# Early score maxima of a fused FNet and multi-query kernel: two key blocks folded into one pass for five query tiles

## Chip, core and metric

The kernel runs on one core of a Trainium2 chip. The metric is the device time of one execution in microseconds. Before the change the median of three runs is 3697.52 us (3696.55 to 3697.98).

## What is computed

Two identical layers, each an FNet mixing sublayer (A) and a multi-query attention sublayer (B), over 2048 rows of 512 numbers:

```python
x = x + A(layernorm(x))   # y = Re(DFT_seq(DFT_hidden(x))): a = x Wre', b = x Wim'; y = Cre a - Cim b
x = x + B(layernorm(x))   # 32 query heads of 16, one key head, one value head
# B: scores = q k' / 4; p = softmax(scores); o = p v; o wo
```

The softmax subtracts the row maximum, so for each of 32 heads and 2048 queries the maximum over 2048 keys is needed before the exponentials.

## The kernel before

**Phase A** of a layer forms the DFT over the sequence for four blocks of 512 output rows. A block is 32 steps: 16 sequence chunks for the real matrix and 16 for the imaginary one. In each step one chunk of the DFT matrix (`craw`, loaded by SP) is split into a high part `ch` (ScalarE, ACT, line 80) and a low part `cl` (GpSimd, POOL, line 81), and TensorE (PE) multiplies it into four PSUM accumulators `x`. From step 48 on (`ROWS`) these matmuls are written as halves of 64 rows (line 650), two of which run side by side; a step is four slots of three such pairs. After 32 steps comes the y stage (line 456 in the halved form), eight units long, with four slots each, and then the preparation of the finished block, spread over the next twelve steps (`prep_tasks`): layer norm, four transposes, keys and values (`do_kv`), and four query projections `q_mm` in the steps 7 to 10 of the next block. Each projection is split into two rows of SBUF, `row4` and `row5` for groups 0 and 2, `row6` and `row7` for 1 and 3, and `q_store` writes these to DRAM (`qd`) with six DMAs one step later (line 347).

**Early maxima.** Since the keys of a finished block are known while later blocks are still in phase A, a part of the row maxima is taken there. The unit of it is a tile of 128 queries and a block of 512 keys: 16 head pairs, for each pair two matmuls (line 361) into PSUM banks `y` and two `reduce_max` on VectorE (DVE, line 362). The table `EARLY` lists (query tile, key block, SBUF slot for the queries, step of their load, start, end). Start and end count 40 positions for a block: 32 steps and the eight y units. The 16 head pairs are placed evenly between them. The banks are `y` (three buffers), `z` (one buffer, also used by the transposes) and `x` (two pairs). Maxima go to `mxe`, for tile 0 straight to its `mxp`.

**Phase B** runs 16 query tiles of 32 steps. A step has four score matmuls (line 817), two exponentials of 1024 columns on ACT (line 820), eight value matmuls in two groups of four (line 831), and some of the maxima not yet taken: `owed(n)` paces them at three a step. They use lines 361 and 362 as well, and write `mxp`.

All engines execute their own instructions in the order of the program. A buffer that is allocated again waits, at its first writer, for every reader of its earlier use, a DMA too, even one that stands later in the program text.

## Time and profile before

| | |
|---|---|
| median of three runs | 3697.52 us |
| the profiled execution | 3699.45 us, span 3697.7 us, granted clock 0.996 |
| layer 1, phase A | about 0 to 700 us |
| layer 1, phase B | about 700 to 1850 us |
| layer 2, phase A | about 1850 to 2500 us |
| layer 2, phase B | about 2500 to 3697 us |
| busy, of the span | PE 98%, DVE 76%, ACT 64%, POOL 25% |

In the views that follow, a row of groups gives line, engine, operation, output and inputs, shapes and count, then busy time and mean nanoseconds of one, then the idle time of the engine just ahead and what ended it. PEld is the weight load of a matmul. A row of the timeline gives start, length, engine, line, operation, tiles and how many follow each other. Reported matmul lengths overlap, so PE's pace is read from starts.

### The profile page before, as it was taken

Reading aid. Unit: us, or ns where it says so; the run is one execution under the profiler, and the core shown is the slowest. Engines: PE = TensorE matmul, PEld = TensorE weight load, DVE = VectorE, ACT = ScalarE, POOL = GpSimd, SP = SyncE. Lnnn points to the kernel's source line nnn. Section 1 sums busy time; section 2 is a strip of 40 time slices with the busy share of each in tenths; the row PEclk is TensorE's granted clock in tenths of the full one; section 3 lists DMA queues with packets and bytes.
Section 4 is the critical chain, followed back from the end, with each engine's and each line's share of the span. In section 5 each row is a group of like instructions: output and inputs, shape, how many; then the busy total and the mean of one; then the engine's idle time right before and its main releaser. Section 6 shows DMA issues by size and latency. Waiting matters only on the chain.

```text
span 3697.7 us, 63649 instructions
## 1 busy us (share of the span) xinstructions
PE 3612.1 (98%) x24672; PEld 1822.8 (49%) x24672; DVE 2817.3 (76%) x4847; ACT 2363.3 (64%) x2974; POOL 915.5 (25%) x1288
## 2 busy tenths in 40 slices
PE   8999999999999999999999999998999999999999
PEld 6866567533333333333377666675333333333333
DVE  6176988688888888888411879886888888888882
ACT  3322221488888888888933231215888888888888
POOL 5534332212112212211254342322111011010101
PEclk9999999999999999999999999999999999999999
DMA  6534233311111100110144242423111111001101
GB/s 189 137 122 148 69 109 92 97 34 34 50 33 36 48 22 25 33 50 22 42 138 121 97 142 69 132 69 101 33 48 36 33 45 39 25 22 47 36 22 27
DMA packets 218047, 247.17 MB, mean 67 GB/s; under 512 B 51664, under 2 KB 173584, under 8 KB 210064
## 3 DMA queue, kind: packets, MB, share of 16 engines
q1 hardware_dynamic: 204048, 225.78, 20.5%
q0 software_dynamic: 13696, 17.33, 1.7%
q8 instruction: 194, 3.18, 0.4%
q14 instruction: 109, 0.89, 0.1%
HBM read 178.77 MB, written 63.17 MB: 65 GB/s over the span
## 4 chain that ended last, share of the span: by engine, by line
PE 90%; DVE 6%; ACT 2%; issue 1%; POOL 1%; DMA 0%; SPq 0%; ACTq 0%; DVEq 0%; POOLq 0%
PE z L831 27%; PE y L361 18%; PE x L817 18%; PE x L650 9%; PE x L456 3%; DVE mxe L362 3%; PE y L89 3%; PE y L91 2%; PE y L90 2%; PE x L91 2%; PE x L90 2%; PE x L89 2%; DVE mxp L362 1%; ACT slot L820 1%; DVE row L183 0%
## 5 line engine op out<-in xcount | busy, mean ns | idle before, releaser
L362 DVE TENSOR_REDUCE mxp<-y 128x1 f32<-128x512 f32 (+1 forms) x3168 | 1972.0, 679 | 229.1 <-PE y L361 208.0
L820 ACT ACTIVATE slot<-x 128x1024 f32<-128x1024 f32 x1990 | 1938.3, 1025 | 295.5 <-PE x L817 278.5
L831 PE MATMUL z<-slot,v 128*32 128x512 f32 x8192 | 1098.0, 606 | 1.5 <-DVE row L835 0.7
L361 PE MATMUL y<-kz,slot 64*128 64x512 f32 (+1 forms) x3360 | 1043.2, 407 | 36.5 <-DVE mxe L362 20.8
L817 PE MATMUL x<-slot,kz 64*128 64x512 f32 x2956 | 675.2, 451 | 9.7 <-DMA slot<-mt 5.8
L362 DVE TENSOR_REDUCE mxe<-y 128x1 f32<-128x512 f32 x960 | 584.3, 682 | 96.2 <-PE y L361 89.2
L817 PEld LDWEIGHTS x<-slot,kz 64*128 64x128 f32 x2956 | 278.5, 184 | 751.8 <-ACT slot L820 677.3
L361 PEld LDWEIGHTS y<-kz,slot 64*128 64x128 f32 x3360 | 484.5, 185 | 236.0 <-DVE mxe L362 166.3
L650 PE MATMUL x<-ch,xnh 64*128 64x512 f32 (+1 forms) x1536 | 411.6, 371 | 5.6 <-DVE row L438 4.2
L650 PE MATMUL x<-ch,xnl 64*128 64x512 f32 (+1 forms) x1536 | 411.3, 371 | 0.0
L650 PE MATMUL x<-cl,xnh 64*128 64x512 f32 (+1 forms) x1536 | 391.4, 354 | 0.0
L81 POOL TENSOR_TENSOR cl<-craw,ch 128x512 fp32r<-128x512 f32 x236 | 300.9, 1297 | 259.4 <-ACT ch L80 232.2
L831 PEld LDWEIGHTS z<-slot,v 128*32 128x32 f32 x8192 | 164.0, 108 | 359.3 <-issue 328.9
L443 ACT CAST xnl<-xnl 128x2 fp32r<-128x2 f32 x160 | 31.2, 195 | 473.6 <-PE x L650 276.4
L650 PEld LDWEIGHTS x<-cl,xnh 64*128 64x128 f32 x1536 | 248.8, 185 | 19.3
L410 POOL DMA_DIRECT2D slot<-mt x208 | 103.3, 504 | 612.8 <-PE y L361 518.8
L650 PEld LDWEIGHTS x<-ch,xnh 64*128 64x128 f32 x1536 | 233.9, 185 | 28.8 <-issue 6.6
L650 PEld LDWEIGHTS x<-ch,xnl 64*128 64x128 f32 x1536 | 234.3, 185 | 19.5 <-issue 4.5
L872 POOL TENSOR_TENSOR row<-row,row 128x256 f32<-128x256 f32 x63 | 46.6, 739 | 686.2 <-DMA row<-rd 661.9
L80 ACT CAST ch<-craw 128x512 fp32r<-128x512 f32 x256 | 147.8, 618 | 39.5 <-DMA craw<-ct_in 13.9
L89 PE MATMUL x<-ch,xnh 128*128 128x512 f32 x384 | 154.8, 403 | 12.2 <-ACT ch L80 9.0
L91 PE MATMUL x<-ch,xnl 128*128 128x512 f32 x384 | 153.5, 400 | 2.0 <-POOL xnl L518 1.8
(168 smaller groups left out, 3131.0 us busy)
## 6 DMA issues: line engine op xcount, KB each, us to landing
craw<-ct_in SPq DMA_DIRECT2D x112, 512.0 KB
slot<-qd SPq DMA_DIRECT2D x48, 1024.0 KB
qd<-row SPq DMA_DIRECT2D x144, 128.0 KB
od<-row SPq DMA_DIRECT2D x252, 64.0 KB
row<-x_in SPq DMA_DIRECT2D x32, 256.0 KB
mid<-row POOLq DMA_DIRECT2D x32, 256.0 KB, 2.3
craw<-ct_in SPq DMA_DIRECT2D x32, 256.0 KB
row<-mid SPq DMA_DIRECT2D x32, 256.0 KB
```

Source lines behind the costliest of these rows:

```text
L80: nc.scalar.copy(hi, raw)
L81: (eng or nc.vector).tensor_sub(lo, raw, f(hi))
L89: nc.tensor.matmul(ps_, ah, bh, start=start, stop=False)
L90: nc.tensor.matmul(ps_, ah, bl, start=False, stop=False)
L91: nc.tensor.matmul(ps_, al, bh, start=False, stop=stop)
L361: nc.tensor.matmul(pm, o.qT[i][gs, pr, :], kz[gs, c0:c0 + n], start=True, stop=True)
L362: nc.vector.reduce_max(to, pm, axis=AX.X)
L456: nc.tensor.matmul(y[:, g ^ h, :], a[cc][gs, k, tt * P:(tt + 1) * P], b[cc][gs, k, :], start=(h, cc, k, u) == (0, 0, 0, 0), stop=(h, cc, k ...
L650: nc.tensor.matmul(z[d], a[gs, s, d * P:(d + 1) * P], b[gs, :], start=first and q < 2 and e == 0, stop=last and q > 1 and e == len(order) - 1)
L817: nc.tensor.matmul(st["e"][:, g, :], kz[64 * g:64 * g + KR, c * P:(c + 1) * P], o.qT[i][64 * g:64 * g + KR, cp:cp + 4, :], start=True, sto ...
L820: nc.scalar.activation(ptiles[i, s_][:, 2 * w:2 * w + 2, :], st.pop("e"), AF.Exp, scale=DH ** -0.5)
L831: nc.tensor.matmul(a[32 * j:32 * j + 32, :], v1[:, c, :], pt[:, j, :], start=c == 0, stop=c == NT - 1)
```

## The change

1. Five query tiles (0, 4, 5, 6, 7) take key blocks 0 and 1 in one go, entries `"f"` of the table. With a difference of keys `kd` = keys of block 0 minus keys of block 1, max(a, b) = b + max(a - b, 0): PE forms a - b into two `y` banks and b into a `y` and the `z` bank, ACT rectifies a - b into `row4` and `row5`, and DVE adds b and takes the maximum in one pass (`tensor_tensor_reduce`). The number of matmuls is the same.
2. `k_diff` forms `kd` once per layer, behind the keys of block 1.
3. The table is rewritten: 12 entries instead of 18, with other starts, ends, slots and loads. Seven single tiles and five folded ones make 17 tiles of maxima in place of 18; (2, 2) goes to phase B. Tile (3, 1) now lies among the folded ones, from 87.25 to 109. Single maxima of odd head pairs use `z` for one of their two banks.
4. The split of the query weights moves from POOL to DVE, has buffers `wh` and `wl` of its own, and is issued behind the projection instead of ahead of it. `ch` and `cl` have four buffers instead of six.
5. Phase B starts with 8 maxima owed instead of 6 and adds one for every 32 steps. Slots for `zh` and `zl` are taken one step later in some places, and the row maxima of tile 14 are made in two halves.

```diff
@@ -33,12 +33,10 @@
 
 
 EARLY = [
-    (0, 0, 2, 44, 56, 61.5), (1, 0, 3, 44, 61.5, 66.5), (2, 0, 2, 54, 66.5, 70.9), (3, 0, 8, 50, 70.9, 87),
-    (0, 1, 0, 66, 87, 91), (1, 1, 1, 66, 91, 94.7), (3, 1, 8, None, 94.7, 98.7),
-    (4, 0, 2, 78, 98.7, 102.7), (4, 1, 2, None, 102.7, 106.7), (5, 0, 3, 78, 106.7, 110.7),
-    (6, 0, 8, 84, 110.7, 116), (6, 1, 8, None, 116, 122.5), (7, 0, 0, 97, 122.5, 126.5),
-    (7, 1, 0, None, 126.5, 130.5), (5, 1, 1, 97, 130.5, 134.6), (2, 1, 2, 108, 134.6, 138.6),
-    (2, 2, 2, None, 138.6, 142.6), (0, 2, 8, 101, 142.6, 148.5),
+    (1, 0, 2, 44, 56, 63.5), (2, 0, 3, 44, 63.5, 70.9), (3, 0, 8, 50, 70.9, 86.5),
+    (0, "f", 0, 66, 87, 95), (3, 1, 8, None, 87.25, 109), (4, "f", 2, 78, 95.5, 103), (5, "f", 3, 78, 103, 110.9),
+    (6, "f", 8, 95, 114, 122), (1, 1, 1, 97, 122.5, 128), (2, 1, 0, 97, 128, 133.9),
+    (7, "f", 2, 108, 134.5, 142.5), (0, 2, 8, 101, 142.5, 148.5),
 ]
 ROWS = 48
 KEPT = [e for e in EARLY if e[0]]
@@ -121,7 +119,7 @@
         return sb.tile([P, 2, 512], F32, name="craw", bufs=3)
 
     def hl_tiles():
-        return (sb.tile([P, 512], F32R, name="ch", bufs=6), sb.tile([P, 512], F32R, name="cl", bufs=6))
+        return (sb.tile([P, 512], F32R, name="ch", bufs=4), sb.tile([P, 512], F32R, name="cl", bufs=4))
 
     wkvh = sb.tile([P, NK, P], F32R, name="wkvh")
     wkvl = sb.tile([P, NK, P], F32R, name="wkvl")
@@ -236,8 +234,8 @@
             nc.sync.dma_start(st["wq", g], wq[:, g, :])
 
         def wq_split(g):
-            st["wqh", g] = hl_tiles()
-            split_sb(st["wq", g], *st["wqh", g], nc.gpsimd)
+            st["wqh", g] = sb.tile([P, 512], F32R, name="wh"), sb.tile([P, 512], F32R, name="wl")
+            split_sb(st["wq", g], *st["wqh", g])
 
         def wq_split_pool(g):
             hi, lo = st["wqh", g] = hl_tiles()
@@ -273,6 +271,19 @@
             for g in range(2):
                 gs = slice(64 * g + 32, 64 * g + 48)
                 nc.vector.tensor_sub(kz[gs, cs], st["pk"][gs], f(kz[gs, cs]))
+
+        def k_diff(tb):
+            if tb == 0:
+                st["kraw"] = sb.tile([P, 512], F32, name="kraw")
+                nc.scalar.copy(st["kraw"], st["pk"])
+                return
+            st["kd"] = kd = sb.tile([P, 512], F32R, name="kd")
+            t = st["kraw"]
+            nc.vector.tensor_sub(t, t, st["pk"])
+            nc.scalar.activation(kd, t, AF.Identity, scale=kmask)
+            for g in range(2):
+                gs = slice(64 * g + 32, 64 * g + 48)
+                nc.vector.tensor_sub(kd[gs], t[gs], f(kd[gs]))
 
         def v_tr(t0, n, vt):
             pv_ = bank("z")[:, :n * 32].rearrange("p (t d) -> p t d", t=n)
@@ -351,23 +362,42 @@
             if i not in o.mxp:
                 o.mxp[i] = sb.tile([P, NPAIR, 2, 4 if i else 5], F32, name=f"mxp{i % 4}")
                 for e, (i_, kb, *_) in enumerate(KEPT):
-                    if i == i_:
-                        nc.gpsimd.tensor_copy(o.mxp[i][:, :, :, kb], st["mxe"][:, e])
+                    for k in (0, 1) if kb == "f" else (kb,):
+                        if i == i_:
+                            nc.gpsimd.tensor_copy(o.mxp[i][:, :, :, k], st["mxe"][:, e])
             return o.mxp[i]
 
-        def max_of(i, pr, g, c0, n, to):
-            pm = bank("y")[:, :n]
+        def max_of(i, pr, g, c0, n, to, tag="y"):
+            pm = bank(tag)[:, :n]
             gs = slice(64 * g, 64 * g + KR)
             nc.tensor.matmul(pm, o.qT[i][gs, pr, :], kz[gs, c0:c0 + n], start=True, stop=True)
             nc.vector.reduce_max(to, pm, axis=AX.X)
+
+        def max_two(i, pr, to):
+            rows = [half(4 + g) for g in range(2)]
+            for k, c in ((st["kd"], 0), (kz, 512)):
+                pm = [bank("z" if c and g else "y") for g in range(2)]
+                for g in range(2):
+                    gs = slice(64 * g, 64 * g + KR)
+                    nc.tensor.matmul(pm[g], o.qT[i][gs, pr, :], k[gs, c:c + 512], start=True, stop=True)
+                for g in range(2):
+                    if c:
+                        nc.vector.tensor_tensor_reduce(rows[g], pm[g], rows[g], 1.0, -3.0e38, ALU.add, ALU.max, to[:, g:g + 1])
+                    else:
+                        nc.scalar.activation(rows[g], pm[g], AF.Relu)
 
         def max_early(e, pr):
             i, kb = EARLY[e][:2]
             if "mxe" not in st:
                 st["mxe"] = sb.tile([P, len(KEPT), NPAIR, 2], F32, name="mxe")
+            if kb == "f":
+                max_two(i, pr, st["mxe"][:, KEPT.index(EARLY[e]), pr] if i else partial(0)[:, pr, :, 0])
+                if i == 0 and pr == NPAIR - 1:
+                    nc.gpsimd.tensor_copy(partial(0)[:, :, :, 1], partial(0)[:, :, :, 0])
+                return
             for g in range(2):
                 to = st["mxe"][:, KEPT.index(EARLY[e]), pr, g:g + 1] if i else partial(0)[:, pr, g, kb:kb + 1]
-                max_of(i, pr, g, kb * 512, 512, to)
+                max_of(i, pr, g, kb * 512, 512, to, "z" if pr % 2 and g else "y")
 
         def max_half(i, pr, g, kb):
             max_of(i, pr, g, kb * 512, 512, partial(i)[:, pr, g, kb:kb + 1])
@@ -562,12 +592,12 @@
             ts[4, 1] = [lambda: tr(2)]
             ts[4] = [lambda: tr(3), lambda: [wq_load(g) for g in range(4)]]
             ts[6, 0] = [do_kv]
-            ts[6, 3] = [lambda: kv_lo(4 * tb, 4)]
+            ts[6, 3] = [lambda: (kv_lo(4 * tb, 4), k_diff(tb) if tb < 2 else None)]
             ts[6] = [lambda: wq_split(0), lambda: v_tr(4 * tb, 4, st["vt"])]
             for g in range(4):
                 ts[7 + g] = [lambda g=g: q_mm(tb, g, *st["xt"])]
                 if g < 3:
-                    ts[7 + g].insert(0, lambda g=g: wq_split(g + 1))
+                    ts[7 + g].append(lambda g=g: wq_split(g + 1))
                 if g:
                     ts[7 + g].append(lambda g=g: q_store(tb, g - 1))
             ts[11] = [lambda: q_store(tb, 3)]
@@ -713,7 +743,7 @@
                     for tt in range(4):
                         x1[tt] = half(tt)
                         nc.sync.dma_start(x1[tt], src[4 * tb + tt])
-                if n in (15, 31, 47, 62, 78, 94, 110, 118):
+                if n in (15, 31, 47, 63, 79, 95, 111, 119):
                     zh[c] = slot(2 * c, F32R).rearrange("p (k t) -> p k t", k=NK)
                     zl[c] = slot(2 * c + 1, F32R).rearrange("p (k t) -> p k t", k=NK)
                 if n < ROWS:
@@ -778,7 +808,7 @@
             for k in range(6):
                 more_max()
 
-        early = {e[:2] for e in EARLY}
+        early = {(e[0], kb) for e in EARLY for kb in ((0, 1) if e[1] == "f" else e[1:2])}
         units = [(0, pr, g, 3) for pr in range(HALF, NPAIR) for g in range(2)]
         units += [(i, pr, g, kb) for i in range(1, NT) for pr in range(NPAIR) for kb in range(4) for g in range(2)
                   if (i, kb) not in early]
@@ -790,7 +820,7 @@
                 o.done += 1
 
         def owed(n):
-            return min(3 * (n + 1) + 6, len(units)) - o.done
+            return min(3 * (n + 1) + 8 + max(n - 13, 0) // NSTEP, len(units)) - o.done
 
         def done_with(i, pr):
             return all(u[:2] > (i, pr) for u in units[o.done:])
@@ -1010,8 +1040,8 @@
                             o.loaded.add(j)
                 for fn in half_tasks(i).get(s_, ()):
                     fn()
-                for at, j, p0, np_ in ((NT - AHEAD, i, HALF, HALF), (NSTEP - AHEAD, i + 1, 0, HALF if i == NT - 2 else NPAIR)):
-                    if j in (0, NT - 1) or j == i + 1 < NT:
+                for at, j, p0, np_ in ((NT - AHEAD, i, HALF, HALF), (NSTEP - AHEAD, i + 1, 0, HALF if i >= NT - 3 else NPAIR)):
+                    if j in (0, NT - 2, NT - 1) or j == i + 1 < NT:
                         if s_ == at:
                             assert done_with(j, p0 + np_ - 1)
                             max_neg_a(j, p0, np_)
```

PE's order near the start of the second half of block 2's steps, before. `y` and `x` are PSUM, `slot2` holds queries of tile 4, `kz` the keys; each L650 row is one pair of halves:

```order
L361 MATMUL y_3832<-kz_70,slot2_3604 128x512
L361 MATMUL y_3835<-kz_70,slot2_3604 128x512
L650 MATMUL x_3678<-ch_3674,xnl_84 128x512 x2
L650 MATMUL x_3678<-cl_3675,xnh_83 128x512 x2
L650 MATMUL x_3678<-ch_3674,xnh_83 128x512 x2
L361 MATMUL y_3844<-kz_70,slot2_3604 128x512
L361 MATMUL y_3847<-kz_70,slot2_3604 128x512
```

Of the change, the same tile, with one head pair of the single tile (3, 1), whose queries are in `slot8`:

```order
L382 MATMUL y_3669<-kd_2937,slot2_3566 128x512
L382 MATMUL y_3670<-kd_2937,slot2_3566 128x512
L382 MATMUL y_3675<-kz_70,slot2_3566 128x512
L382 MATMUL z_3676<-kz_70,slot2_3566 128x512
L680 MATMUL x_3653<-ch_3497,xnh_83 128x512 x2
L680 MATMUL x_3653<-cl_3498,xnh_83 128x512 x2
L680 MATMUL x_3653<-ch_3497,xnl_84 128x512 x2
L680 MATMUL x_3653<-ch_3501,xnh_83 128x512 x2
L680 MATMUL x_3653<-cl_3502,xnh_83 128x512 x2
L680 MATMUL x_3653<-ch_3501,xnl_84 128x512 x2
L373 MATMUL y_3694<-kz_70,slot8_1766 128x512
L373 MATMUL z_3697<-kz_70,slot8_1766 128x512
```

Before, each slot ends with one head pair of one key block; now every second slot ends with one head pair of two key blocks, whose last matmul needs the only `z` bank.

ACT's order in the change at the first two query projections of block 1, with what each instruction waits for (`row4_2991` and `row5_2992` belong to a folded head pair, `row4_3024` is the high part of a projection, DMAHW are DMAs that must have landed):

```order
L387 ACTIVATE row4_2991<-y_2993 128x512 [waits PE_49]
L387 ACTIVATE row5_2992<-y_2994 128x512 [waits PE_49]
L82 ACTIVATE row0_3026<-y_3011 128x512 [waits PE_49,Activation_49]
L83 CAST row4_3024<-row0_3026 128x512 [waits DVE_49,Activation_49]
L78 CAST wh_3030<-row1_2847 128x512 [waits DMAHW0_49]
L78 CAST ch_3036<-craw_2785 128x512 [waits DMAHW6_49]
L78 CAST ch_3040<-craw_2785 128x512
L387 ACTIVATE row4_3050<-y_3052 128x512 [waits DMAHW2_49,DMAHW5_49,DMAHW1_49,DMAHW6_49,PE_49,Pool_49]
L387 ACTIVATE row5_3051<-y_3053 128x512 [waits DMAHW0_49,DMAHW7_49,DVE_49,PE_49]
```

Before, nothing but casts stood behind the projection's split; now the rectify that follows it writes `row4` again and waits for the six DMAs of `q_store`. The same holds two projections later.

On DVE one folded head pair is four instructions, two passes and behind each the read of its maximum:

```order
L385 ISA row4_2991,mxp0_2958<-y_2999,row4_2991 128x512
L385 ISA mxp0_2958 128x1
L385 ISA row5_2992,mxp0_2958<-z_3000,row5_2992 128x512
L385 ISA mxp0_2958 128x1
```

These take the place of four `reduce_max` of 128x512.

## Prediction

> **What bounds the kernel now.** First the page's busy line and its slices.

> ```profile
> PE 3612.1 (98%) x24672; PEld 1822.8 (49%) x24672; DVE 2817.3 (76%) x4847; ACT 2363.3 (64%) x2974; POOL 915.5 (25%) x1288
> ...
> PE   8999999999999999999999999998999999999999
> DVE  6176988688888888888411879886888888888882
> ```

> PE looks full everywhere, so the share says nothing about who sets the pace. The groups do: the weight loads of the maxima's matmuls wait for the reductions, most in phase A (`mxe`).

> ```profile
> L361 PEld LDWEIGHTS y<-kz,slot 64*128 64x128 f32 x3360 | 484.5, 185 | 236.0 <-DVE mxe L362 166.3 <-DVE mxp L362 42.9 <-DVE row L893 7.0
> ```

> Next the paces, from two timelines of phase A: PE where maxima are sparse (with the DVE row there), and DVE where they are dense.

> ```profile
> 262.40 0.40 PE L361 MATMUL y<-kz,slot 64*128 64x512 f32 x2
> 262.64 2.92 PE L456 MATMUL x<-slot,slot 64*128 64x512 f32 x24
> 265.39 0.40 PE L361 MATMUL y<-kz,slot 64*128 64x512 f32 x2
> ...
> 262.83 1.29 DVE L362 TENSOR_REDUCE mxe<-y 128x1 f32<-128x512 f32 x2 [2.36 <-PE y L361]
> ...
> 351.72 6.66 DVE L362 TENSOR_REDUCE mxe<-y 128x1 f32<-128x512 f32 x11
> ```

> Thirteen pairs of halves take 265.39 - 262.40 = 2.99 us, 0.23 a pair: a slot of three pairs is 0.69. A result reaches DVE 0.43 after its matmul's start. Reductions follow each other every (6.66 - 0.68) / 10 = 0.60. One head pair in every slot asks 1.20 of DVE and 0.92 of PE, so in dense stretches DVE sets the pace. The windows of line 362 (length, DVE busy, count; 32 a tile) show where:

> ```profile
> 195.40:256.30 60.90, 58.40 (x97) 1.00 0.37 131
> 256.30:316.40 60.10, 20.55 (x33) 0.97 0.30 106
> 316.40:368.80 52.40, 40.18 (x67) 1.00 0.52 141
> 368.80:446.40 77.60, 76.13 (x128) 1.00 0.24 82
> 446.40:496.70 50.30, 38.79 (x64) 0.97 0.21 74
> 496.70:574.50 77.80, 58.76 (x97) 1.00 0.47 129
> 574.50:614.40 39.90, 38.43 (x66) 1.00 0.25 81
> ```

> By their counts these stretches are the table's positions 56, 70.9, 87, 95, 110.7, 122.5, 134.6 and 142.6. I price layer 1 and double it.

> **The folded head pair.** No row shows the combined pass. The nearest are these:

> ```profile
> L438 DVE TENSOR_TENSOR row<-y,row 128x512 f32<-128x512 f32 x12 | 8.3, 692 | 87.9 <-PE y L91 87.9
> L81 DVE TENSOR_TENSOR slot<-row,slot 128x512 fp32r<-128x512 f32 x16 | 16.4, 1035 | 25.1 <-ACT slot L80 25.1
> L942 DVE TENSOR_SCALAR lnv<-mv 128x1 f32<-128x1 f32 x16 | 2.3, 145 | 0.0
> L84 ACT ACTIVATE row<-y 128x512 f32<-128x512 f32 x24 | 14.4, 599 | 109.6 <-issue 82.7 <-PE y L91 13.9 <-POOL cl L81 13.0
> ```

> The pass adds PSUM to SBUF as L438 does: 0.69, started 0.60 apart as reductions are. The read of its maximum I take as 0.10, between nothing and L942's 0.145. DVE needs 1.4 a head pair for two key blocks, where four reductions need 2.4. That gain is real, but the new work is a chain and `z` is one buffer. From the first matmul at 0: rectifies 0.43 to 1.03 and, 0.52 later (two casts of 0.62 in 1.14, below), to 1.55; first pass 1.06 to 1.75; second 1.76 to 2.45, its read to 2.55. Only then is `z` free, and PE, being in order, holds two slots (1.38) behind the next head pair's last matmul. A late bank also exposes a weight load, 0.19 by the group above and 0.05 of handover. With period p, that matmul starts at 2.55 - p + 0.24 and ends 0.23 later, and the next head pair follows 1.38 after that: p = 1.38 + 0.23 + 0.24 + 2.55 - p, **p = 2.2** against 1.84 (eight pairs) at PE's pace and 2.4 before. With the read free it is 2.15; without overlap of passes, and 0.15 for the read, 2.3.

> [...]

> A single head pair among folded ones (tile (3, 1)) puts two reductions, 1.20, between the passes and delays a bank by that plus 0.24: 1.44, where PE alone would need 0.23.

> **The waits for `q_store`.** The first folded tile lies on positions 87 to 95, where the four projections of block 1 are. Before, there:

> ```profile
> 320.27 0.47 PE L89 MATMUL y<-slot,ch 128*128 128x512 f32 x1 [0.20 <-DVE mxp L362]
> ...
> 323.18 0.50 PE L650 MATMUL x<-ch,xnh 64*128 64x512 f32 x2
> ...
> 323.33 0.60 ACT L84 ACTIVATE row<-y 128x512 f32<-128x512 f32 x1 [6.90 <-issue]
> 323.97 0.62 ACT L85 CAST row<-row 128x512 fp32r<-128x512 f32 x1
> 324.49 1.14 ACT L80 CAST ch<-craw 128x512 fp32r<-128x512 f32 x2
> ...
> 324.61 3.94 SPq L347 DMA_DIRECT2D qd<-row  x6
> ...
> mid<-row POOLq DMA_DIRECT2D x32, 256.0 KB, 2.3
> ...
> qd<-kz POOLq DMA_DIRECT2D x32, 128.0 KB, 3.8
> ```

> A projection takes 2.9 on PE. Its six DMAs are all issued 5.4 after its end (328.55 - 323.18), and land, by the two nearest rows, 2.3 to 3.8 later. The rectify behind it writes `row4` and waits for them: 7.7, then 0.60 and 0.24 until PE has a bank, 8.5 in all. On ACT every later cast and rectify stands behind it, on DVE the passes and reductions, and PE runs out of `y` banks after three slots and one head pair, some 2.5. So PE stands 6 us, twice (groups 0 and 2): 12, between 0 (if other waits cover it) and 15. SP runs ahead and is not held.

> **The sum for a layer.**
> - Positions 56 to 70.9: two single tiles in 59.6 slots, 41.1 + 32 x 0.23 = 48.5 at PE's pace, some 50 with uneven spacing, DVE 38: -11.
> - 87 to 95: 16 x 2.2 + four projections 11.6 + six singles 8.6 + 12 = 67.4 against 52.4: +15.
> - 95 to 110.9: 32 x 2.2 + 12 x 1.44 = 87.7 against 77.6: +10. Before, 3.9 tiles of one key block stood here; now it is 4.7.
> - 110.7 to 122.5: 14.4 slots 9.9 + 16 x 2.2 = 35.2, and 3 for the row sums of the y stage that enter DVE between the passes: 48 against 50.3: -2.
> - 122.5 to 134.6: two single tiles instead of three, with 285 halves 32.8, 60 full matmuls 13.8, transposes 2, maxima 7.4 on PE, and 8 kept for the preparation's waits: 64 against 77.8: -14.
> - 134.6 to 142.6: 16 x 2.2 + 1 = 36 against 39.9: -4.
> - `kd`: behind the keys of block 1 come a subtraction (0.69), a scaling and two small subtractions before the first folded matmul:

> ```profile
> L262 ACT ACTIVATE kz<-y,kone,kmask 128x512 fp32r<-128x512 f32 (+1 forms) x10 | 6.9, 694 | 38.0 <-PE y L91 38.0
> L275 DVE TENSOR_TENSOR kz<-y,kz 16x512 fp32r<-16x512 f32 (+1 forms) x20 | 11.7, 584 | 48.7 <-ACT row L265 48.4
> ```

>   0.69 + 0.69 + 2 x 0.58 = 2.6 later than the keys alone; about 2 of it is uncovered: +2.
> - Casts of `ch` (1.14 every two steps) stand ahead of rectifies; I take 0.05 a folded head pair: +4. The weight split behind the projection has one buffer, with a step (2.8) to cover some 2.9: +1. Four instead of six `ch` buffers still leave two steps for 1.2 of casts and 2.6 of POOL: 0. POOL's eight subtractions less, the later `zh` and the copies of `mxe` lie beside other work: 0.
> - Phase B gets tile (2, 2), 32 maxima more. Its step, before:

> ```profile
> 1299.99 0.40 PE L817 MATMUL x<-xnh,kz 64*128 64x512 f32 x2
> 1300.24 0.39 PE L361 MATMUL y<-kz,slot 64*128 64x512 f32 x1
> 1300.56 1.07 PE L831 MATMUL z<-slot,v 128*32 128x512 f32 x8
> ...
> 1301.56 0.50 PE L817 MATMUL x<-xnh,kz 64*128 64x512 f32 x2
> ```

>   The third maximum runs alone for 0.32, so a fourth beside it costs little; 16 pairs of 0.23 are 3.7: +4, from 0 to 32 x 0.60 = 19 if DVE set the pace there.

> Together -11 + 15 + 10 - 2 - 14 - 4 + 2 + 4 + 1 + 4 = **+5 a layer, +10 in all**. The profiled execution took 3699.45 us (span 3697.7), so it would be 3709; the median shown is 2 lower, so **3708 us**. The spread of single tiles wins, the folded tiles where a fifth one is squeezed in lose it again. The sum is even at p = 2.2 - 5/80 = 2.14, close by.

> **Rivals.**
> - *The chain is hidden* (other side: not slower). If `z` came free within 1.83 of the head pair's first matmul instead of 2.55 (2 x 1.84 - 1.38 - 0.23 - 0.24 = 1.83), PE would not stop and p would be 1.84; below 2.14 the change wins. For it speaks DVE's load, 1.4 in 1.84; against it the single `z` buffer and the order of PE. Then 87 to 95 takes 42.5 (-10), 95 to 110.9 61 (-16), 110.7 on 42 (-8), 134.6 on 29.5 (-10); with -11, -14, +2 and +4: -63 a layer, 3572; with the `q_store` waits kept -51, 3596. Chance 12%; in between, 3615 to 3680, 14%.
> - *The pass is dearer*: if it costs L81's 1.035 instead of 0.69, the chain is 0.69 longer, p 2.55, 80 head pairs a layer 28 more: 3763. 12%. For it: L81 adds two tensors and is that slow at times. Against: L438 reads PSUM, as the pass does, and is not. [...]
> - *More than one of these, or later landings of `q_store`*: above 3740, 7%.

> **How the numbers follow.** The forecast (3680 to 3740) has 55%, of it 5% below 3690, 15% up to 3705, 35% above. 0.2%, 7.4 us, is about what a measurement of this kernel tells from no change. Faster: 12 + 14 + 5 = 31%; the same 15%; slower 35 + 12 + 7 = 54%. The range leaves out the strongest gain and the worst sums: 3615 to 3775.

> **What would show it.** In the changed profile: combined passes of 0.69 and reads near 0.10; between folded head pairs starts 2.2 apart with weight loads of line 382 waiting for DVE; two idle stretches of some 6 us on ACT's line 387 that end with `qd` landing, around the projections; 56 to 70.9 in 50 us; phase B 4 us longer. Folded head pairs 1.84 apart, or no waits at `row4`, would make the forecast wrong.

## The result, and the profile after

The changed kernel takes 3729.51 us (median of 4 runs, 3726.0 to 3735.91) where the kernel before takes 3697.68 (3696.55 to 3697.98): ratio 1.0089, 95% interval 1.0071 to 1.0106. It is slower by 32 us; 3708 was forecast, with a range of 3615 to 3775.

The page of the changed kernel, its busy line and the granted clock in slices:

```profile
PE 3597.7 (96%) x24672; PEld 1864.2 (50%) x24672; DVE 2681.5 (72%) x4885; ACT 2544.0 (68%) x3288; POOL 899.2 (24%) x1280
...
PEclk9998999999999999999999989999999999999999
```

VectorE has less to do (72% for 76%), ScalarE more (68% for 64%), as the fold intends. TensorE is busy 14 us less in a span that is 32 longer. The mean granted clock of the profiled execution is 0.986 over a span of 3729.8 us; before it was 0.996 over 3697.7. Time at missing clock is (1 - 0.986) x 3729.8 = 52 us against 15. Not all of that costs time (PE waits in some of it anyway), but it is more than the whole loss, and no term of the prediction speaks of it. The four runs of the changed kernel rank by their clock: 3726.0 us at 0.989, 3727.42 at 0.988, 3731.59 at 0.986 and 3735.91 at 0.985.

Where the time went is read by cutting phase A at the same steps in both traces (a block is 32 steps and eight y units, so that step 71 is position 87, step 79 is 95, step 98 about 122.5, step 110 about 134):

| stretch | before, layers 1 and 2 | after, layers 1 and 2 | difference | forecast |
|---|---|---|---|---|
| steps 48 to 63 (two spread single tiles) | 62.2, 62.2 | 50.5, 50.5 | -11.7, -11.7 | -11 |
| 71 to 79 (first fold, four projections) | 52.8, 52.8 | 75.1, 75.2 | +22.3, +22.4 | +15 |
| 79 to 95 (folds with tile (3, 1)) | 77.8, 77.8 | 79.4, 79.4 | +1.6, +1.6 | +10 |
| 95 to 98 with the y stage | 47.2, 46.0 | 45.2, 46.6 | -2.0, +0.6 | -2 |
| 98 to 110 (single tiles, preparation) | 77.4, 77.3 | 74.4, 78.8 | -3.0, +1.5 | -14 |
| 110 to 120 | 61.3, 61.3 | 56.7, 58.7 | -4.6, -2.6 | -4 |
| phase B | 1142.2, 1141.0 | 1149.1, 1148.1 | +6.9, +7.1 | +4 |

Layer 2 begins at 1853.4 us before and at 1864.3 after, so layer 1 is 11 us longer and layer 2 is 21 us longer, though both run the same program.

Rows of the windows of before, for three of these stretches in layer 1 and its phase B. A row gives start and end, length, busy time and count of PE, PEld, DVE, ACT, POOL, then granted clock, DMA share, GB/s:

```profile
core 0: us, PE busy (x) PEld busy (x) DVE busy (x) ACT busy (x) POOL busy (x), PEclk, DMA share, GB/s
...
315.20:346.90 31.70, 31.19 (x180) 20.70 (x178) 19.80 (x33) 8.57 (x19) 13.89 (x11) 1.00 0.42 92
...
368.00:445.80 77.80, 76.09 (x512) 44.36 (x514) 77.54 (x130) 14.99 (x38) 22.75 (x18) 1.00 0.24 82
...
493.00:570.40 77.40, 74.91 (x464) 48.56 (x461) 60.74 (x100) 21.73 (x47) 33.48 (x30) 1.00 0.46 126
...
710.60:1852.80 1142.20, 1136.36 (x7759) 425.85 (x7760) 955.34 (x1681) 996.70 (x1087) 235.33 (x486) 1.00 0.14 40
```

The same stretches of the changed kernel, with steps 48 to 63 ahead of them and steps 98 to 110 of layer 2 behind:

```profile
194.50:245.00 50.50, 50.12 (x427) 40.08 (x428) 41.37 (x65) 14.87 (x36) 22.89 (x18) 1.00 0.40 144
302.60:355.60 53.00, 39.00 (x184) 26.43 (x182) 21.42 (x46) 18.23 (x36) 9.67 (x7) 0.81 0.25 55
...
377.70:457.10 79.40, 73.92 (x536) 51.47 (x534) 56.15 (x153) 49.03 (x102) 22.41 (x19) 1.00 0.21 74
...
502.30:576.70 74.40, 65.49 (x437) 47.53 (x435) 48.71 (x77) 22.86 (x49) 26.77 (x23) 0.98 0.42 109
...
714.70:1863.80 1149.10, 1144.43 (x7791) 429.15 (x7790) 974.18 (x1715) 996.57 (x1082) 238.67 (x493) 1.00 0.14 39
...
2353.50:2432.30 78.80, 70.17 (x436) 50.75 (x433) 48.77 (x77) 22.81 (x49) 26.62 (x22) 0.91 0.40 105
```

Steps 71 to 75 stand out: 53.0 us instead of 31.7 with nearly as many matmuls, PE idle for 14.0 of them, and the clock at 0.81, so 0.19 x 53 = 10 us at missing clock. Steps 98 to 110 differ by 4.4 us between the two layers, and there the clock differs too: 0.02 x 74.4 = 1.5 missing in layer 1, 0.09 x 78.8 = 7 in layer 2. The timeline of steps 71 to 75 shows the wait that was forecast, and what came behind it:

```profile
315.24 3.95 SPq L358 DMA_DIRECT2D qd<-row  x6
...
321.24 1.09 ACT L387 ACTIVATE row<-y 128x512 f32<-128x512 f32 x2 [4.47 <-DMA qd<-row]
321.87 0.69 DVE L385 CUSTOM_DVE_ANT_0 row<-y,row 128x512 f32<-128x512 f32 x1 [4.73 <-ACT row L387]
...
321.89 1.28 PE L382 MATMUL y<-kd,slot 64*128 64x512 f32 x2 [5.27 <-ACT row L387]
...
322.63 0.79 PE L382 MATMUL y<-kz,slot 64*128 64x512 f32 x1
```

The rectify stands 4.47 us until the six DMAs have landed, PE 5.27 until the rectify has freed a `y` bank. Then matmuls that take 0.39 elsewhere take 0.79.

The fold itself, in the view of its line: counts, shortest, median and longest nanoseconds, and who waited how long.

```profile
L385 DVE DVE_READ_ACCUMULATOR2_ANT mxe<- x256: 81/83/86, 383.4 to 2474.9; 128x1 f32 x128
L385 DVE CUSTOM_DVE_ANT_0 row<-y,row x160: 678/692/694, 306.8 to 2473.7; 128x512 f32<-128x512 f32 x160
...
  ACT row L387: 140.9, 98
...
  PEld z L382: 27.5, 80
```

The pass takes 0.692 and the read 0.083, as assumed (0.69 and 0.10); VectorE waits 140.9 us for rectifies, and 80 weight loads for `z`.

Two waits are new that the prediction did not name. In steps 98 to 110 the waits of PE (total, times, longest) show transposes, L248, behind reductions of single maxima, because odd head pairs now hold `z`:

```profile
PE z L248 <- DVE mxe L374: 4.7, 4, 1.9
PE y L373 <- DVE mxe L374: 2.0, 3, 1.1
PE z L291 <- DVE mxe L374: 1.5, 1, 1.5
```

And VectorE, in the same stretch, stands idle in front of the weights' subtraction until ScalarE has cast the high part, which comes behind the projection. Three subtractions (here of line 79) wait 4.2, 3.6 and 3.2 us, 11.1 in all, and what is ready for VectorE stands behind them:

```profile
L79 DVE TENSOR_TENSOR wl<-row,wh x3: 1370/1370/1428, 543.5 to 560.3; 128x512 fp32r<-128x512 f32 x3
...
  ACT wh L78: 11.1, 3
```

### The profile page after: what moved, and what is told of

It reads as the page before. It is cut to its first block, busy times and chain, and to the rows that moved or that the text cites. A ratio compares the mean times of both kernels' runs of the same rounds, so it can differ in the third digit from the quotient of the medians.

```text
span 3729.8 us, 64663 instructions
## 1 busy us (share of the span) xinstructions
PE 3597.7 (96%) x24672; PEld 1864.2 (50%) x24672; DVE 2681.5 (72%) x4885; ACT 2544.0 (68%) x3288; POOL 899.2 (24%) x1280
## 5 line engine op out<-in xcount | busy, mean ns | idle before, releaser
L374 DVE TENSOR_REDUCE mxp<-y 128x1 f32<-128x512 f32 (+1 forms) x3088 | 1923.1, 678 | 200.2 <-PE y L373 187.1
L373 PE MATMUL y<-kz,slot 64*128 64x512 f32 (+1 forms) x2608 | 716.0, 398 | 13.6 <-DVE mxe L374 4.1
L373 PEld LDWEIGHTS y<-kz,slot 64*128 64x128 f32 x2608 | 343.9, 188 | 63.0 <-DVE mxp L374 22.6
L680 PE MATMUL x<-ch,xnh 64*128 64x512 f32 (+1 forms) x1536 | 349.5, 371 | 6.9 <-DVE row L468 4.7
L680 PE MATMUL x<-cl,xnh 64*128 64x512 f32 (+1 forms) x1536 | 347.6, 363 | 0.0
L680 PE MATMUL x<-ch,xnl 64*128 64x512 f32 (+1 forms) x1536 | 346.7, 370 | 0.0
L387 ACT ACTIVATE row<-y 128x512 f32<-128x512 f32 x320 | 176.0, 596 | 130.0 <-PE y L382 46.1
L374 DVE TENSOR_REDUCE mxe<-y 128x1 f32<-128x512 f32 x288 | 187.9, 685 | 92.0 <-PE y L373 45.1
L385 DVE CUSTOM_DVE_ANT_0 row<-y,row 128x512 f32<-128x512 f32 x160 | 110.7, 692 | 166.0 <-ACT row L387 140.9
L680 PEld LDWEIGHTS x<-cl,xnh 64*128 64x128 f32 x1536 | 213.8, 192 | 19.8
L680 PEld LDWEIGHTS x<-ch,xnl 64*128 64x128 f32 x1536 | 207.9, 192 | 25.1 <-issue 4.5
## 6 DMA issues: line engine op xcount, KB each, us to landing
qd<-row SPq DMA_DIRECT2D x144, 128.0 KB
row<-x_in SPq DMA_DIRECT2D x32, 256.0 KB
mid<-row POOLq DMA_DIRECT2D x32, 256.0 KB, 2.3
craw<-ct_in SPq DMA_DIRECT2D x32, 256.0 KB
row<-mid SPq DMA_DIRECT2D x32, 256.0 KB
```

Of the source, the lines that this page charges most:

```text
L373: nc.tensor.matmul(pm, o.qT[i][gs, pr, :], kz[gs, c0:c0 + n], start=True, stop=True)
L374: nc.vector.reduce_max(to, pm, axis=AX.X)
L385: nc.vector.tensor_tensor_reduce(rows[g], pm[g], rows[g], 1.0, -3.0e38, ALU.add, ALU.max, to[:, g:g + 1])
L387: nc.scalar.activation(rows[g], pm[g], AF.Relu)
L680: nc.tensor.matmul(z[d], a[gs, s, d * P:(d + 1) * P], b[gs, :], start=first and q < 2 and e == 0, stop=last and q > 1 and e == len(order) - 1)
```

## The experiments

Theory T: the fold works, as a chain that holds `z`, with a period near 2.1; the loss comes from a few new waits at fixed places (rows of `q_store`, `z` for single maxima, the weights on VectorE), each with its own length and with a stretch of half clock behind it. Rival R: the folded stretches are limited by the work of VectorE and ScalarE or by phase B, and a wait that is taken away only shows up elsewhere. Each experiment has its own rival condition in its expectation. Ratios are to the kernel before, run beside it on the same chip. Kernels are compared with each other by their ratios, times 3698 us; the interval of a ratio is about ±0.0012, so such a difference is good to some ±6 us (±8 with the changed kernel).

| run | median us | before beside it | ratio | 95% interval |
|---|---|---|---|---|
| changed kernel | 3729.51 | 3697.68 | 1.0089 | 1.0071 to 1.0106 |
| e1_qrows | 3706.52 | 3699.68 | 1.0015 | 1.0006 to 1.0024 |
| e2_y | 3716.39 | 3699.68 | 1.0043 | 1.0031 to 1.0055 |
| e3_fill | 3718.76 | 3699.68 | 1.0052 | 1.0040 to 1.0064 |
| e4_tile22 | 3701.0 | 3699.68 | 1.0001 | 0.9992 to 1.0009 |
| e5_both | 3694.01 | 3701.9 | 0.9975 | 0.9964 to 0.9985 |
| e6_nofold | 3813.34 | 3701.9 | 1.0297 | 1.0283 to 1.0312 |
| e7_pipe | 3678.37 | 3701.9 | 0.9932 | 0.9919 to 0.9944 |
| e8_wqpool | 3684.73 | 3701.9 | 0.9952 | 0.9938 to 0.9965 |
| e9_best | 3663.46 | 3698.38 | 0.9907 | 0.9893 to 0.9920 |
| e10_stops | 3728.34 | 3698.38 | 1.0078 | 1.0066 to 1.0091 |
| e11_wqpool_after | 3721.24 | 3698.38 | 1.0060 | 1.0047 to 1.0074 |

**e1_qrows: rows of their own for the projections of block 1.**

```diff
-            hi = half(4 + 2 * (g % 2), F32R)
-            lo = half(5 + 2 * (g % 2), F32R)
-            split_act(pq, hi, lo, half(g))
+            at = ((6, 7), (0, 1), (2, 6), (3, 7))[g] if tb == 1 else (4 + 2 * (g % 2), 5 + 2 * (g % 2))
+            hi = half(at[0], F32R)
+            lo = half(at[1], F32R)
+            split_act(pq, hi, lo, f(lo) if tb == 1 and g else half(g))
```

> The changed kernel, but the four projections of block 1 write rows of their own (row6/row7, row0/row1, row2/row6, row3/row7) instead of row4 and row5, so that no rectify waits for q_store; the maxima and the fold are untouched. Theory T (waits and the clock behind them): in each layer the two idle stretches of 5.3 us on PE at the projections go, and with them the half-clock stretches that follow (10.2 us of lost clock in steps 71 to 75); steps 71 to 75 fall from 53.0 us to 33 to 38, the whole time by 30 to 40 us to about 3690 to 3700. By the waits alone, without the clock, it would fall by 20 to 22. Rival R (the fold's passes and the load of DVE set the pace there, and the wait only stands where another would): steps 71 to 75 stay above 46 and the time falls by less than 10.

3706.52; by the ratios (1.0089 - 1.0015) x 3698 = 27 us less than the changed kernel, 23 by the medians. Steps 71 to 75 in both layers, then the waits of PE there in layer 1:

```profile
303.00:348.40 45.40, 40.60 (x185) 27.45 (x184) 21.37 (x46) 18.11 (x36) 9.73 (x7) 0.81 0.29 64
...
2142.00:2184.50 42.50, 37.72 (x186) 25.53 (x184) 21.36 (x46) 18.11 (x36) 9.74 (x7) 0.88 0.31 68
```

```profile
PE y L383 <- DVE kd L286: 1.7, 2, 1.5
PE y L383 <- ACT row L388: 1.3, 2, 0.7
PE z L374 <- DVE mxp L386: 0.9, 1, 0.9
```

The two long stops are gone, and the time falls by the four of them (21) and a little more. R is out by the total time, though its bound of 46 us for steps 71 to 75 is missed by only 0.6 in layer 1. T's size is missed too: 42 to 45 us remain, not 33 to 38. Stops of 0.5 to 1.5 us are left (the key difference, the rectify behind a projection's casts), and the clock is still 0.81 and 0.88. The largest single cause is shown, and it is smaller than I expected of it.

**e2_y: single early maxima on `y` alone.**

```diff
-                max_of(i, pr, g, kb * 512, 512, to, "z" if pr % 2 and g else "y")
+                max_of(i, pr, g, kb * 512, 512, to)
```

> The changed kernel, but single early maxima use y banks alone, as before the change; the fold keeps its one matmul into z. Theory T: the transposes of the preparation no longer wait for a reduction that holds z; the idle stretches of 1.9, 0.5, 0.6, 1.65 and 1.5 us in steps 98 to 104 go, and most of the lost clock that follows them, above all in layer 2 (27 us lost in its phase A): 8 to 25 us less in all, most of it in steps 98 to 110 of layer 2. Rival R: three y banks are too few for singles among folded head pairs, so steps 79 to 95 become longer by as much as 98 to 110 gain: within 5 us of the changed kernel.

3716.39; 17 us less by the ratios, 13 by the medians. Steps 98 to 104 fall from 39.3 and 42.1 to 34.5 at full clock. But 104 to 110 grow from 35.1 and 36.7 to 40.3, at a clock of 0.92, in both layers:

```profile
531.70:572.00 40.30, 35.31 (x214) 25.02 (x215) 22.98 (x34) 11.23 (x24) 13.52 (x10) 0.92 0.51 117
...
2378.20:2418.50 40.30, 35.31 (x214) 24.91 (x215) 22.92 (x34) 11.20 (x24) 13.53 (x10) 0.92 0.50 117
```

The waits of PE in the first of these windows say why:

```profile
PE y L373 <- DVE mxe L374: 4.8, 3, 1.8
```

Without `z` the single maxima run out of banks sooner while VectorE stands at the weights. T holds for the transposes; what R expected (too few banks) happens too, at the projections and not among the folds, where 79 to 95 became 1.3 shorter.

**e3_fill: work instead of a stop.** Behind the matmuls of two folded head pairs:

```diff
+                for g in range(2 * 22 if c and i == 0 and pr in (2, 6) else 0):
+                    gs = slice(64 * (g % 2), 64 * (g % 2) + KR)
+                    nc.tensor.matmul(pm[g % 2], o.qT[i][gs, pr, :], k[gs, c:c + 512], start=True, stop=True)
```

> The changed kernel with 22 extra pairs of matmuls (5.1 us at 0.23 a pair) at two head pairs of tile 0's fold in each layer, put where PE stands still behind the waits for q_store; they write the banks that are then written again by the real matmuls, so the results are the same and only work is added. If the clock falls because PE stands still (theory T), PE now stays busy there and the half-clock stretches behind go: steps 71 to 75 fall from 53.0 to 42 to 48 us, the whole time falls by 8 to 20 us although 88 pairs of matmuls are added. If the lost clock has another cause (the power of the pass, the load of DVE), the time stays or grows by 0 to 10 us and the half-clock stretches stay.

3718.76; 14 us less by the ratios, 11 by the medians, although 88 pairs of matmuls were added. The window of steps 71 to 75:

```profile
304.30:353.20 48.90, 44.85 (x274) 31.44 (x272) 21.41 (x46) 18.32 (x36) 9.79 (x7) 0.97 0.28 60
```

ScalarE waits as before, and PE does useless work meanwhile; 53.0 us become 48.9 (T expected 42 to 48), and the clock goes from 0.81 to 0.97. In this window the half clock comes from PE standing still, and costs on its own at least those 4 us a layer.

**e4_tile22: the kernel before with tile (2, 2) in phase B.**

```diff
-    (2, 2, 2, None, 138.6, 142.6), (0, 2, 8, 101, 142.6, 148.5),
+    (0, 2, 8, 101, 142.6, 148.5),
...
-            return min(3 * (n + 1) + 6, len(units)) - o.done
+            return min(3 * (n + 1) + 8 + max(n - 13, 0) // NSTEP, len(units)) - o.done
...
+                for at, j, p0, np_ in ((NT - AHEAD, i, HALF, HALF), (NSTEP - AHEAD, i + 1, 0, HALF if i >= NT - 3 else NPAIR)):
+                    if j in (0, NT - 2, NT - 1) or j == i + 1 < NT:
```

> The kernel before, with nothing but this of the change: tile 2 of key block 2 is no longer taken early, phase B starts with 8 maxima owed instead of 6 and adds one every 32 steps, and tile 14's row maxima come in two halves. Theory T: phase B is 7 us longer in each layer, as in the changed kernel, the stretch 138.6 to 142.6 of phase A about 8 to 10 shorter, together between -6 and 0 us against the kernel before. Rival R (the 7 us of phase B are not its maxima but a consequence of phase A's change): phase B stays within 2 us of before, the total falls by 14 to 20 us.

3701.0, ratio 1.0001, no difference. Its windows of steps 110 to 120 (61.3 before) and of phase B (1142.2 before):

```profile
569.20:621.90 52.70, 49.53 (x528) 40.85 (x527) 32.70 (x56) 11.20 (x28) 13.23 (x11) 1.00 0.24 79
701.00:1850.60 1149.60, 1143.82 (x7791) 428.17 (x7790) 974.58 (x1716) 997.04 (x1082) 239.62 (x493) 1.00 0.14 39
```

It gives 8.6 in phase A and takes 7.4 in phase B, with no fold anywhere. So the 7 us a layer of phase B are the price of 32 maxima there, 7.4 / 32 = 0.23 each, and R is out for this part.

**e5_both: both cures, e1 and e2.**

> Both cures together: the projections of block 1 write rows of their own, and single early maxima use y banks alone. If the two waits stand at different places and each carries its own lost clock (theory T), the gains add: 23 and 13 us less than the changed kernel, 3690 to 3697 us, and with less lost clock in phase A of layer 2 than either alone. If one of them only shifts the stall to the other (rival R), the time stays at 3700 or above.

3694.01, ratio 0.9975: faster than the kernel before, 42 us less than the changed kernel, where the two alone gave 27 and 17. Within these errors they add.

**e6_nofold: the same places, without folding** (four reductions for a head pair, no key difference):

```diff
-                max_two(i, pr, st["mxe"][:, KEPT.index(EARLY[e]), pr] if i else partial(0)[:, pr, :, 0])
+                for k in range(2):
+                    for g in range(2):
+                        at = len(KEPT) + FOLDED.index(i) if i and k else KEPT.index(EARLY[e]) if i else 0
+                        max_of(i, pr, g, k * 512, 512,
+                               st["mxe"][:, at, pr, g:g + 1] if i else partial(0)[:, pr, g, k:k + 1])
```

> As the kernel with both cures, with the same table of places, but each folded head pair is taken as two plain key blocks (four matmuls with the keys themselves into y, four reductions on VectorE), with no key difference and no work on ScalarE. Theory T (folding itself shortens a head pair where VectorE is dense, from 2.4 to about 2.1 us): 80 head pairs a layer of 0.27 more are 22, less 2 to 5 for the key difference and its lost clock: 30 to 45 us longer than with the fold, 3720 to 3740. Rival R (the chain of fold, rectify and pass eats what VectorE saves): within 8 us of the kernel with both cures.

3813.34, 119 us more than with the fold: T's sign, at three times its size. Steps 79 to 95 of e5_both, then of e6_nofold:

```profile
364.80:442.80 78.00, 72.02 (x533) 54.38 (x531) 55.64 (x153) 49.83 (x102) 22.33 (x19) 1.00 0.22 78
```

```profile
374.20:476.20 102.00, 86.90 (x534) 55.61 (x532) 92.77 (x152) 16.45 (x38) 22.67 (x18) 0.97 0.18 61
```

VectorE is busy 92.77 of 102.0 without the fold. I had compared with the dense pace of before, 2.4 a head pair of two blocks, and forgot that this table puts single head pairs among them: 32 head pairs of 2.4 and 10 of 1.2 are 89 us for VectorE alone. That four matmuls in a burst into three banks also make the work less even is not shown. This run is no copy of the kernel before, so it says that this table needs the fold, not that the fold is worth 119 us.

**e7_pipe: passes one slot later.** As e5_both, with the head pair's second half at a later place:

```diff
+                    for c in (0, 512) if kb == "f" else (0,):
+                        at = divmod(int(4 * (n1 + pr * (n2 - n1) / NPAIR)) + c // 512, 4)
...
+                        inner.setdefault(at, []).append(lambda e=e, pr=pr, c=c: max_early(e, pr, c))
```

> As the kernel with both cures, but of each folded head pair the matmuls with the keys of block 1 and the two passes are issued one slot (three pairs of halves) after the matmuls with the key difference and the rectifies, so that z is taken later and freed sooner after it. Theory T (the chain through the one z bank and the order of PE sets the period of 2.1): the period falls towards 1.85 where only folded head pairs stand (steps 96 to 98 and 110 to 120), less in steps 79 to 95, where VectorE is nearly full; 10 to 20 us a layer, 20 to 40 in all, 3655 to 3675 us. Rival R (the period is set by the work of VectorE and ScalarE in the stretch, whatever the order): within 8 us of the kernel with both cures.

3678.37, 16 us less than e5_both by ratios and medians, less than the 20 to 40 expected. Where only folded head pairs stand, the period shows as the distance of passes that read `z`. In the changed kernel (VectorE, steps 112 to 118):

```profile
594.42 0.69 DVE L385 CUSTOM_DVE_ANT_0 row<-z,row 128x512 f32<-128x512 f32 x1
...
596.98 0.69 DVE L385 CUSTOM_DVE_ANT_0 row<-z,row 128x512 f32<-128x512 f32 x1
...
598.86 0.69 DVE L385 CUSTOM_DVE_ANT_0 row<-z,row 128x512 f32<-128x512 f32 x1
...
600.92 0.69 DVE L385 CUSTOM_DVE_ANT_0 row<-z,row 128x512 f32<-128x512 f32 x1
```

and in e7_pipe:

```profile
583.73 0.69 DVE L388 CUSTOM_DVE_ANT_0 row<-z,row 128x512 f32<-128x512 f32 x1
...
585.59 0.69 DVE L388 CUSTOM_DVE_ANT_0 row<-z,row 128x512 f32<-128x512 f32 x1
...
587.46 0.69 DVE L388 CUSTOM_DVE_ANT_0 row<-z,row 128x512 f32<-128x512 f32 x1
...
589.33 0.69 DVE L388 CUSTOM_DVE_ANT_0 row<-z,row 128x512 f32<-128x512 f32 x1
```

2.56, 1.88 and 2.06 become 1.86, 1.87 and 1.87: PE's pace. The 2.56 still follows a disturbed start of the tile. Behind it 1.8 to 1.9 and 2.0 to 2.1 alternate, about 1.97 in the mean, in the changed kernel and in e5_both alike, so the order alone gives 0.1 a head pair here. There the order of work made the period, not the work. Steps 79 to 95 gain only 1.8 (78.0 to 76.2) with VectorE busy 56 of 76, so T was wrong to expect more there and wrong on the reason (a full VectorE). The waits show `y` banks held by single maxima there, 4.7 us of PE; what else limits that stretch stays open, and so does the way in which the 16 us divide among the stretches.

**e8_wqpool and e11_wqpool_after: the weights' low part on GpSimd again**, the first on top of e5_both, the second in the changed kernel:

```diff
-            split_sb(st["wq", g], *st["wqh", g])
+            split_sb(st["wq", g], *st["wqh", g], nc.gpsimd)
```

> As the kernel with both cures, with the low part of the query weights made by GpSimd again instead of VectorE, in the same place of the program. Theory T: the subtractions of 0.7 to 1.4 us on VectorE stand ahead of folded passes at the projections of block 1 and cost about 1 us each there, with their lost clock 0 to 3 a layer; the time falls by 0 to 8 us. Rival R: GpSimd, which also splits the DFT matrix, is then late with cl or with the weights themselves, and the time grows by 2 to 10 us.

> The changed kernel with one part undone: GpSimd makes the low part of the query weights again, in the same place of the program and in the new buffers; everything else is as changed. Theory T (on VectorE that subtraction waits 3.2 us for the cast of the weights' high part, and reductions or passes that are ready stand behind it, in all four projections): steps 104 to 110 fall from 35.1 and 36.7 to about 32, and the time falls by 6 to 14 us from the changed kernel's 3729.5. Rival R (in the changed kernel the other waits cover it): within 4 us of 3729.5.

e8: 3684.73, 9 us less than e5_both, just past the 0 to 8 that T allowed. e11: 3721.24, 11 us less than the changed kernel by the ratios, 8 by the medians. Both at the place expected in the second text, steps 104 to 110, and not at the projections of block 1, which I had named in the first. Here e5_both, e8 and e11:

```profile
524.20:563.20 39.00, 34.00 (x214) 24.07 (x215) 22.94 (x34) 11.22 (x24) 13.53 (x10) 0.96 0.52 120
```

```profile
523.00:555.00 32.00, 31.81 (x212) 23.08 (x213) 19.13 (x31) 11.19 (x24) 16.47 (x13) 1.00 0.62 144
```

```profile
544.90:574.90 30.00, 30.00 (x213) 23.85 (x214) 19.16 (x31) 11.35 (x24) 16.45 (x13) 1.00 0.65 149
```

PE goes from 5.0 us of idle time to 0.2 and 0.0. In steps 32 to 48, where no early maxima stand behind the weights, GpSimd costs 2.1 to 2.2 a layer against VectorE (62.6 to 64.7 or 64.8).

**e9_best: e7 with e8, and tile 0's fold three slots later** (87.75 to 95.25):

```diff
-    (0, "f", 0, 66, 87, 95), (3, 1, 8, None, 87.25, 109), (4, "f", 2, 78, 95.5, 103), (5, "f", 3, 78, 103, 110.9),
+    (0, "f", 0, 66, 87.75, 95.25), (3, 1, 8, None, 87.25, 109), (4, "f", 2, 78, 95.5, 103), (5, "f", 3, 78, 103, 110.9),
```

> As the kernel with both cures and the folded pass one slot later, with the low part of the query weights made by GpSimd, and tile 0's fold from 87.75 to 95.25 instead of 87 to 95, so that the key difference is ready before its first matmul. Theory T (each of these waits costs its own length and the lost clock behind it, and they stand at different places): 9 us less for GpSimd, as measured without the later pass, and 2 x (1.5 + 1.7) = 6 less for the key difference: 3678 - 15 = 3663, between 3656 and 3670. Rival R (VectorE is full in steps 71 to 95 anyway, so what is saved at one place is waited for at the next): 3671 or above.

3663.46, ratio 0.9907: 34 us faster than the kernel before and 67 than the changed one. The median is where T put it, but the kernel before ran 3.5 us faster on this chip than beside e7_pipe; by the ratios the gain on e7_pipe is 9 us and not 15, between T and R. Steps 71 to 75 fell from 39.1 in both layers to 35.7 and 34.2, 75 to 79 grew by 1.6.

**e10_stops: the kernel before, with stops of PE.** `STOP = {4: 1, 8: 2, 12: 3, 18: 1, 22: 2, 26: 5}`, and at the end of such a step:

```diff
+                if n in STOP:
+                    for c in (STOP[n], 0):
+                        pm = bank("z")
+                        nc.tensor.matmul(pm, xnh[:, s, :P], ch, start=True, stop=True)
+                        for _ in range(c):
+                            nc.scalar.copy(pm, pm)
```

> The kernel before with six deliberate stops of PE in steps 4 to 27 of each layer, where its trace shows full clock and no early maxima: a matmul into z, then 1, 2, 3, 1, 2 or 5 copies of that bank onto itself on ScalarE, then a second matmul into z that waits for them; nothing reads the result. By the copies (0.6 us each, some 0.25 of handover) PE stands 0.85, 1.45, 2.05, 0.85, 1.45 and 3.25 us, 9.9 a layer, 20 in all. Theory T (a stop of about 1.5 us or more is followed by a stretch of 3.4 us at half clock): behind the stops of 1.45 and more the clock halves in most cases, 1.7 us lost each time, so 4 stops a layer give 10 to 14 us on top: 3727 to 3737. Rival R (the half clock in the changed kernel comes from the passes or the mix of engines there, not from the stops): clock stays full in these steps and the time grows by 16 to 22 us, 3714 to 3722.

3728.34, 30 us more by the medians, 29 by the ratio. The six stops measure 0.66, 1.31, 1.92, 0.66, 1.99 and 3.12 in layer 1, the same in layer 2 but for 1.32 in place of 1.31 and of 1.99: 9.7 + 9.0 = 18.7. Around the third stop of layer 1, three windows of 3.4 us, then PE's timeline:

```profile
53.80:57.20 3.40, 1.48 (x8) 0.86 (x6) 2.34 (x3) 1.77 (x4) 0.99 (x1) 1.00 0.66 145
57.20:60.60 3.40, 3.40 (x8) 2.72 (x9) 2.38 (x2) 2.55 (x5) 2.83 (x4) 0.50 0.34 39
60.60:64.00 3.40, 3.40 (x16) 2.73 (x16) 1.87 (x2) 0.00 (x0) 1.63 (x3) 1.00 0.80 257
```

```profile
54.88 0.40 PE L746 MATMUL z<-ch,xnh 128*128 128x512 f32 x1
57.19 0.80 PE L746 MATMUL z<-ch,xnh 128*128 128x512 f32 x1 [1.92 <-ACT z L748]
57.79 0.63 PE L90 MATMUL x<-ch,xnh 128*128 128x512 f32 x1
...
60.70 0.39 PE L91 MATMUL x<-cl,xnh 128*128 128x512 f32 x1
```

After a stop of 1.92 us PE starts 8 matmuls in 3.4 us instead of 16. In both layers this follows the stops of 1.92 and 3.12, and never those of 0.66, 1.31 or 1.32; the one of 1.99 was not followed by it. So R is out: the stops of 1.92 and 3.12 us alone bring half clock here, with no fold in the program. T is right in the sum: stops of 18.7 us, and five stretches at half clock behind them, 8.5 us of lost clock, are 27, measured 29 to 30. Its bound of about 1.5 us is too low at this place.

## Why the prediction came out as it did

The forecast had the sign and the main mechanism; its sum was +10 where 32 came. That the time still lies in the likeliest band, 3680 to 3740, is in part luck, for errors of both signs cancel in it. By the prediction's own steps:

- *Positions 56 to 70.9, -11*: -11.7 in both layers. Right.
- *The folded head pair, p = 2.2*: pass, read and chain as assumed (second read ended 2.41 after the first matmul in the head pair at 309.33, forecast 2.55). In the changed kernel the median period without a single head pair is 2.09 in steps 79 to 95, the mean 2.33; where folded head pairs are alone and undisturbed it is 1.97, between the forecast and PE's pace. For that last case e7_pipe shows that the late `z` and PE's order set it. The second pass starts 0.61 after the first (594.42 and 593.81), forecast 0.60, and the read lies between.
- *The waits for `q_store`, 6 us twice a layer*: idle times of 5.27 and 5.50 in layer 1, 5.20 and 5.23 in layer 2, ended by the DMAs. Right in place and cause. The stretch 71 to 79 came out at +22 against 15, with some 4 more priced in other terms (the key difference, casts, weights). Up to 12 us a layer there is lost clock, for which the prediction had no term. **The step that failed is that a wait was priced at its length alone.** e3_fill and e10_stops show the rest.
- *Positions 95 to 110.9, +10*: +1.6. The single head pair among folded ones was priced at 1.44 and costs 0.34 (medians 2.43 and 2.09): its two reductions fall into time in which VectorE waits for rectifies anyway (140.9 us in all), while I put them into the chain in full. The sum also counts too many: six single head pairs up to position 95 and twelve behind it are 18, where the tile has 16, and the trace has ten behind 95. So 2 x 1.44 + 10 x 1.10 = 14 us a layer are too many, of which the mean period of 2.33 instead of 2.2 takes back 4.
- *122.5 to 134.6, -14*: -3.0 and +1.5. **Here "8 kept for the preparation's waits" failed**: it took the waits of before, while the change makes new ones, `z` for single maxima and the weights on VectorE. With both taken away and the order of e7_pipe, steps 98 to 110 take 65.7 in e9_best (483.8 to 549.5), 11.7 less than before.
- *Weight split behind the projection, +1*: e11_wqpool_after gives 4 to 5 a layer. The text counted VectorE's time and the buffer's cover, but not who is queued behind an instruction that waits 3.2 to 4.2 us for its input.
- *`kd`, +2*: PE stands 1.51 us; right, without the half clock that follows at 305.9.
- *Phase B, +4*: +7; right in kind, 7 / 32 = 0.22 a maximum instead of 0.115, and the same in e4_tile22.
- *110.7 to 122.5 and 134.6 to 142.6, -2 and -4*: -2.0 and -4.6 in layer 1; in layer 2 +0.6, at a clock of 0.96 against 1.00, and -2.6, for which the clock (0.97 in both) is no reason.

A layer came out 8 lower than forecast in the folds with tile (3, 1), 11 to 15 higher in the preparation, some 3 higher in the first fold with its extra terms, and 3 higher in phase B; so 10 in all became 32. Of the rivals, the hidden chain did not occur, though 1.97 comes near it, and e7_pipe reaches it where folded head pairs are alone; the dearer pass is out, at 0.69. By the three undone parts (27, 17 and 11; 51 together in e8_wqpool against the changed kernel) the change without its three new waits is 18 us faster than the kernel before.

## What to carry to other kernels

The new operation was not the cost here (0.692 us a pass, as assumed); the buffers that it borrows were (27 us less in e1_qrows, 17 in e2_y). For each row, bank and queue that an edit begins to share, ask which slow reader (a DMA, a reduction) it now waits for and what stands behind it in order. A producer and its consumer issued one slot apart instead of back to back brought PE back to its own pace here (1.87 us a head pair in e7_pipe for about 1.97). And a stop of TensorE is to be priced with the half-clock stretch that may follow: here stops of 1.51 and 1.92 us were followed by 3.41 us at 0.5, others of 1.65 and 1.99 were not.

## What the runs showed of the hardware

Two stops of PE in the changed kernel, the first followed by half clock at 305.9, the second not:

```profile
305.09 0.49 PE L382 MATMUL y<-kd,slot 64*128 64x512 f32 x1 [1.51 <-DVE kd L286]
...
520.25 0.65 PE L248 MATMUL z<-ident,row 128*128 128x128 f32 x4 [1.65 <-DVE mxe L374]
```
